# Seven products instead of eight for eleven hidden blocks of a state-space scan followed by a gated feed-forward layer

## The chip, the core and the metric

The kernel runs on one core of one Trainium2 chip. The core has TensorE (PE, matrix products into the accumulator memory PSUM), VectorE (DVE), ScalarE (ACT), GpSimd (POOL) and SyncE (SP, which issues DMA transfers here). Each engine works through its own queue in order, and the queues wait for one another through semaphores. Weight loads of TensorE have a row of their own in the profile (PEld). The metric is the device time of one execution in microseconds, as the median of several runs. All data is fp32.

## The reference: what is computed

First a chunked state-space scan (Mamba-2) over 4 batches, 8 heads, 768 positions, 32 channels a head and a state of 16. Its output, laid out as 3072 tokens of 256 numbers, goes through a feed-forward layer with a cosine gate:

```
M = (C_i . B_j) * exp(cum_i - cum_j), causal
y = M @ x + (C @ state) * exp(cum)          # per chunk, then the state is carried on
x = y as (3072, 256)
h = x @ w_in            # w_in  (256, 2048)
g = h * cos(h)
out = g @ w_out         # w_out (2048, 256)
```

## The kernel before

**Chunks and steps.** The sequence is cut into NC = 6 chunks of 128 positions (512 tokens over the four batches). The scan gives `yT[c]`, the transposed scan output of chunk c, as two halves u of 256 tokens each, with the 256 channels in two blocks k of 128. The feed-forward layer goes over each chunk in NF = 16 steps; step n = 16c + f. A step is one half u and one pair j of hidden blocks: 256 hidden numbers (two blocks e of 128) for 256 tokens (two blocks of 128). In the last chunk, steps 80 to 87 are the first half and 88 to 95 the second.

**What a step does.** `first(n)` (L650, products at L659) makes hp, the hidden block before the gate: four products of 256 columns into one PSUM bank, laid out as two blocks e by 256 tokens. It is eight block products of 128x128x128. `wind_k` (L664, ACT) rounds hp/2pi to whole turns k, `wind_w` (L669, DVE) takes the fraction w, `gate` (L679, ACT) turns w into the cosine, and `gated` (L683, DVE) multiplies it with hp into gT. Then `second(n - LAG)`, with LAG = 2, multiplies the gT of two steps ago with w_out.

**The second half in seven products.** From chunk 1 on, `second` is `seven` (L739). It forms the eight block products of a step out of seven (the scheme of Strassen and Winograd). For that it needs differences of the blocks of w_out, made once by POOL (`differ_w`, L695), and of the blocks of gT, made in every step by POOL (`differ`, L707: `gd`, three operations). The seven products are summed over the eight steps of a half in PSUM (`o[c, u]`). After the last of them ACT copies the accumulators out (`ps`, L776 and L777), four DVE adds (L784) put the output together, and SP writes it (L787). These adds wait in the list `unsummed` and are issued in a later step. The last step of all, 95, is done in plain products (`last_step`, L807), onto accumulators laid out for it.

**What sets the order.** The program is written with a manual schedule: each engine runs its instructions in the order in which the loop at L999 issues them. In a step of the last chunk that is: products of hp (PE), k (ACT), w (DVE), cosine (ACT), gT (DVE), differences of gT (POOL), then the adds of `unsummed` if they are due, then the seven products of step n - 2 (PE).

**PSUM.** It has eight banks: two for hp (tag "h"), two for accumulators (tag "o"), and two pairs (tag "scan") that serve the scan and are free once the scan of the last chunk is done. With two hp banks, gT of step n has to be made before hp of step n + 2 begins.

**SBUF used again.** `ms` are four buffers of 1024 numbers a partition. The scan uses the first two to its end, the other two only early on. The buffers with tag "words" held pieces of the weights while they were read in.

Of the kernel before, what the change touches and what calls it, by code (L numbers as in the profile page):

```python
# [8 lines left out]
FP32 = mybir.dt.float32  # L9
U32 = mybir.dt.uint32  # L10
I32 = mybir.dt.int32
AF = mybir.ActivationFunctionType
ALU = mybir.AluOpType
# [12 lines left out]
def kernel(  # L26
# [13 lines left out]
    V, ACT, G, PE = nc.vector, nc.scalar, nc.gpsimd, nc.tensor  # L40
# [3 lines left out]
    P = 128  # L44
    NC = S // P
    DM, DF = moe_w_in.shape
    KT = DM // P
    NF = DF // P
    TB = NB * P
# [3 lines left out]
    LAG = 2  # L53
# [15 lines left out]
    def bank(shape, name, tag):  # L69
        return psum.tile(shape, FP32, tag=tag, bufs=2, name=name)  # L70

    def pair(name):

        return psum.tile([P, 2, 4 * P], FP32, tag="scan", bufs=2, name=name)
# [570 lines left out]
    def turn_of(n):  # L645

        c, f = divmod(n, NF)
        return (f % 2, f // 2) if c == 0 else divmod(f, NJ)

    def first(n, between=None, tag="h"):  # L650
        c, f = divmod(n, NF)
        hp[n] = bank([P, TB], "hp", tag) if tag else pair("hp")[:, 0]

        u, j = turn_of(n)
        to_, y = hp[n].rearrange("p (e i) -> p e i", e=2), yT[c][:, u]
        for e in range(2):
            fs = slice((2 * j + e) * P, (2 * j + e + 1) * P)
            for k in range(KT):
                PE.matmul(to_[:, e], lhsT=w_in[:, k, fs], rhs=y[:, k],  # L659
                          start=(k == 0), stop=(k == KT - 1), skip_group_check=True)  # L660
            if between and e == 0:
                between()

    def wind_k(n):  # L664
        k = ffn.tile([P, TB], I32, tag="k", name="k")
        ACT.activation(k, hp[n], AF.Copy, bias=0.25, scale=INV_2PI)  # L666
        turns[n] = k

    def wind_w(n):  # L669
        k = turns[n]  # L670
        turns[n] = w = ffn.tile([P, TB], FP32, tag="w", name="w")
        V.scalar_tensor_tensor(out=w, in0=hp[n], scalar=INV_2PI, in1=k,  # L672
                               op0=ALU.mult, op1=ALU.subtract)

    def wind(n):
        wind_k(n)
        wind_w(n)

    def gate(n):  # L679
        cos = turns[n]  # L680
        ACT.activation(cos, cos, AF.Sin, bias=quarter, scale=TWO_PI)  # L681

    def gated(n):  # L683
        cos = turns.pop(n)
        gT[n] = ffn.tile([P, TB], FP32, tag="gT", bufs=LAG + 1, name="gT")
        V.tensor_tensor(out=gT[n], in0=hp.pop(n), in1=cos, op=ALU.mult)  # L686
        gT[n] = gT[n].rearrange("p (q m) -> p q m", q=4)
        if NF <= n < NC * NF - 1:
            differ(n)
# [5 lines left out]
    def differ_w(i, js):  # L695

        if i == len(wd):
            t = conv.tile([P, 2 * WC, 2], U32, tag="words", bufs=8, name="words")
            wd.append(t.rearrange("p a w -> p (a w)").bitcast(FP32)
                      .rearrange("p (j m) -> p j m", j=NJ))  # L700
        w11, w12, w21, w22 = (w4[:, js, e, h] for e in range(2) for h in range(2))
        a_ = (w12, w22, w22, w21)[i]
        b_ = (w11, w12, wd[0][:, js], wd[min(i, 2)][:, js])[i]
        op = ALU.add if i in (1, 2) else ALU.subtract
        G.tensor_tensor(out=wd[i][:, js], in0=a_, in1=b_, op=op)

    def differ(n):  # L707
# [5 lines left out]
        G.tensor_tensor(out=d[:, 2], in0=g[:, 0], in1=d[:, 0], op=ALU.subtract)  # L713
        G.tensor_tensor(out=d[:, 3], in0=g[:, 2], in1=d[:, 2], op=ALU.subtract)  # L714

    unit_rows = out.rearrange("(s q k i) m -> q k i s m", s=2, q=2, i=W)

    def second(n):
# [20 lines left out]
    def seven(n):  # L739

        c = n // NF
        u, j = turn_of(n)
        final = n >= NC * NF - NJ
        if j == 0:


            if final:
                lo, hi = (pair("o")[:, 0].rearrange("p (q m) -> p q m", m=P) for _ in range(2))
                mid = bank([P, 4, P], "o", "o")
                o[c, u] = (mid, lo, hi, {1: mid[:, 0], 6: mid[:, 1], 7: mid[:, 2], 5: mid[:, 3],  # L750
                                         2: lo[:, 0], 3: lo[:, 1], 4: hi[:, 0]})
            else:
                lo, hi = (bank([P, 4, P], "o", "o") for _ in range(2))
                o[c, u] = (lo, hi, {1: lo[:, 0], 6: lo[:, 1], 2: lo[:, 2], 7: hi[:, 0],
                                    5: hi[:, 1], 4: hi[:, 2], 3: hi[:, 3]})
        at = o[c, u][-1]
        g = gT.pop(n)
        if n == NC * NF - 1:
            last_step(g, *o[c, u][1:3])
            return  # L760
        d = gd.pop(n)
        w = {1: w4[:, j, 0, 0], 2: w4[:, j, 1, 0], 3: w4[:, j, 1, 1], 4: wd[3][:, j],
             5: wd[0][:, j], 6: wd[2][:, j], 7: wd[1][:, j]}
        a_ = {1: g[:, 0], 2: g[:, 2], 3: d[:, 3], 4: g[:, 3], 5: d[:, 0], 6: d[:, 2], 7: d[:, 1]}
        starts = (1, 2, 4) if final else (1, 7)
        for q in (1, 2, 6, 7, 5, 4, 3):
            PE.matmul(at[q], lhsT=a_[q], rhs=w[q], start=(j == 0 and q in starts),  # L767
                      stop=(j == NJ - 1), skip_group_check=True)
        if final and j == NJ - 2:
            shared(o[c, u][0])  # L770
        if j < NJ - 1:
            return

        sum_ = two.tile([P, 7, P], FP32, tag="sum", bufs=1, name="sum")
        ps = two.tile([P, 7, P], FP32, tag="ps", bufs=1, name="ps")
        ACT.copy(out=ps[:, 0:3], in_=o[c, u][0][:, 0:3])  # L776
        ACT.copy(out=ps[:, 3:7], in_=o[c, u][1])  # L777

        def rest():
            for dst, a_, b_ in ((sum_[:, 0:2], ps[:, 1:3], ps[:, 0:1]),  # L780
                                (sum_[:, 5:7], ps[:, 3:5], sum_[:, 0:1]),
                                (sum_[:, 3:5], ps[:, 5:3:-1], sum_[:, 5:6]),
                                (sum_[:, 2:3], ps[:, 6:7], sum_[:, 6:7])):
                V.tensor_tensor(out=dst, in0=a_, in1=b_.to_broadcast([P, dst.shape[1], P]),  # L784
                                op=ALU.add)
            for s in range(2):
                nc.sync.dma_start(out=unit_rows[s, 2 * c + u], in_=sum_[s * W:(s + 1) * W, 1:5].rearrange(  # L787
                                      "p (t h) m -> p t (h m)", t=2))

        unsummed.append(rest)  # L790

    unsummed = []
    shares_ = {}

    def shared(mid):
# [146 lines left out]

    AHEAD = 4

    def first_steps():

        grade("in", 1)
        for q in range(2):
            weights(1, q)
        states_of = []  # L950
        first(0, lambda: states_of.extend(finish0(1)))
        take_s1, add_s1 = states_of
        join("in", 1)
        rests = [grade("out", 0, later=True)]
        wind_k(0)
        take_s1()
        rests.pop()()
        wind_w(0)
        first(1)
        join("out", 0)  # L960
        wind_k(1)
        gate(0)
        wind_w(1)
        gate(1)
        gated(0)
        gated(1)
        first(2, tag=None)
        rests = [grade("in", 2, later=True)]
        wind_k(2)
        rests.pop()()  # L970
        clip_cut()
        wind_w(2)
        rests = [grade("out", 1, later=True)]
        join("in", 2)
        first(3, tag=None)
        gate(2)
        wind_k(3)
        rests.pop()()
        rests = [grade("in", 3, later=True)]
        gated(2)  # L980
        join("out", 1)
        second(0)
        wind_w(3)
        gate(3)
        rests.pop()()
        rests = [grade("out", 2, later=True)]
        join("in", 3)
        gated(3)
        second(1)
        clip_all()  # L990
        return add_s1, rests
# [7 lines left out]
    for n in range(AHEAD, NC * NF + LAG):  # L999
        c, f = divmod(n, NF)  # L1000
        if n < NC * NF:
# [10 lines left out]
                load_along(2, (2 * (n == NF), 2 * (n == NF) + 1))  # L1012
            for e, i in chunks_at(n, "along"):
                load_along(e + 1, (2 * i, 2 * i + 1))
            first(n)
            closing = f == NF - 1 and 1 <= c < NC - 1
            take_y = finish2(c + 1) if closing else None
            wind(n)
            if closing:
                take_y(0)  # L1020
            for e, s in chunks_at(n - 1, "turn"):
# [2 lines left out]
                turn_unit(k)  # L1024
            if n + 1 in piece:
                rests_of.append(grade(*piece[n + 1], later=True))
            gate(n)
            while len(rests_of) > (n == AHEAD):
                rest = rests_of.pop(0)
                if rest:  # L1030
# [14 lines left out]
            behind = [lambda k=k: weights(k, 1) for k in units_at(n - 1, 3)] + behind  # L1045
            if not joins and behind:
                behind.pop(0)()
            gated(n)
            if closing:
                take_y(1)  # L1050
            if n == NF + 7:
# [5 lines left out]
                exchange()  # L1057
            for do in behind:
                do()
            if f not in ((10, 11, 12) if c == 1 else (10, 11)):  # L1060
                for do in unsummed:
                    do()
                unsummed.clear()
# [2 lines left out]
                    weigh0(k)  # L1066
        for i, js in differ_at.get(n, ()):
            differ_w(i, js)
        if n == AHEAD + 1:
            second(AHEAD - LAG)  # L1070
        if n >= LAG and n != AHEAD:
# [53 lines left out]
```

## Time and profile before

| | |
|---|---|
| median of three runs | 368.21 us (367.43 to 368.46) |
| profiled execution, its own time | 367.37 us |
| its span, first to last instruction | 365.2 us |
| TensorE busy | 359.7 us (98%) |
| weight loads | 324.8 us (89%) |
| DVE busy | 249.6 us (68%) |
| POOL busy | 204.5 us (56%) |
| ACT busy | 177.8 us (49%) |
| granted TensorE clock, mean | 0.999 |
| hp of the last chunk's steps starts | at 305.36, then every 3.29 us |

In a line of the profile L659 is the line of the kernel, `hp<-yT,w_in` names the output and the inputs, x8 is a count. In groups, the busy time and the mean duration in nanoseconds follow, then the idle time of the engine just before and what ended it. In a timeline the first two numbers are start and duration in microseconds. Where a line of a timeline stands for several instructions, its duration is the sum or the union of theirs. Matmuls overlap one another, so the chain, which lays them end to end, gives the time that they take of TensorE.

### The profile page before, as it was taken

To read this page: it belongs to the slowest core of one execution; us is meant where nothing else is said; L and a number is where in the kernel's file an instruction comes from. 1 tells how busy PE (TensorE), PEld (TensorE's weight loads), DVE (VectorE), ACT (ScalarE), POOL (GpSimd) and SP (SyncE) were. 2 spreads that over 40 slices of the span, in tenths; PEclk is the share of its full clock that TensorE was granted. 3 is DMA by queue.
4 is the path that set the end of the run, shared out by engine and by line. 5 is a ranking of instruction groups with operands and counts; after the bars stand their busy time and mean duration, and the time that the engine had idled before them with its cause. 6 is when DMAs were issued, how large, how long until landed. Compare 5 with 4: busy or idle time off the path is not lost.

```text
span 365.2 us, 9749 instructions
## 1 busy us (share of the span) xinstructions
PE 359.7 (98%) x3902; PEld 324.8 (89%) x3902; DVE 249.6 (68%) x420; ACT 177.8 (49%) x324; POOL 204.5 (56%) x331
## 2 busy tenths in 40 slices
PE   8999999999999999999999999999999999999995
PEld 5788888888999999999989999989999999999995
DVE  7799998488868747967735977754876363644463
ACT  4588766454454355534345444335553534443442
POOL 6567666679766544447734456744355443554441
PEclk9999999999999999999999999999999999999999
DMA  8997865692664455316034210010000010010011
GB/s 146 294 334 154 203 139 72 105 129 64 133 98 65 92 106 72 69 39 121 9 56 62 47 50 22 2 44 5 22 11 0 2 31 2 2 29 3 0 29 31
DMA packets 97324, 26.39 MB, mean 72 GB/s; under 512 B 87328, under 2 KB 93184, under 8 KB 97280
## 3 DMA queue, kind: packets, MB, share of 16 engines
q1 hardware_dynamic: 96032, 25.38, 34.6%
q8 instruction: 31, 0.51, 0.6%
q10 hardware_dynamic: 1248, 0.39, 0.5%
q14 instruction: 13, 0.11, 0.1%
HBM read 22.36 MB, written 3.34 MB: 70 GB/s over the span
## 4 chain that ended last, share of the span: by engine, by line
PE 89%; DVE 4%; POOL 3%; ACT 2%; issue 2%; ACTq 0%; POOLq 0%; DVEq 0%
PE hp L659 42%; PE o L767 33%; PE o L729 5%; PE y L629 2%; PE g L603 1%; PE y L477 1%; DVE mag L261 1%; PE y L617 1%; DVE mag L263 1%; POOL gd L711 1%; PE g L456 1%; PE a_ps L364 1%; PE warm L84 1%; DVE w L672 1%; POOL gd L713 1%
## 5 line engine op out<-in xcount | busy, mean ns | idle before, releaser
L659 PE MATMUL hp<-yT,w_in 128*128 128x256 f32 x768 | 182.7, 381 | 0.3 <-DVE gT L686 0.3
L659 PEld LDWEIGHTS hp<-yT,w_in 128*128 128x128 f32 x768 | 139.5, 190 | 18.2 <-issue 1.0
L711 POOL TENSOR_TENSOR gd<-gT 128x256 f32<-128x256 f32 x79 | 59.8, 757 | 111.9 <-DVE gT L686 102.5
L672 DVE SCALAR_TENSOR_TENSOR w<-hp,k 128x512 f32<-128x512 f32 x96 | 66.1, 688 | 71.4 <-ACT k L666 71.3
L681 ACT ACTIVATE w<-w,quarter 128x512 f32<-128x512 f32 x96 | 69.4, 723 | 71.8 <-DVE w L672 71.5
L666 ACT ACTIVATE k<-hp 128x512 int32<-128x512 f32 x96 | 57.2, 596 | 94.3 <-PE hp L659 94.1
L686 DVE TENSOR_TENSOR gT<-hp,w 128x512 f32<-128x512 f32 x96 | 65.6, 683 | 35.1 <-ACT w L681 33.2
L767 PE MATMUL o<-words,gd 128*128 128x128 f32 x474 | 65.9, 275 | 0.1
L767 PEld LDWEIGHTS o<-words,gd 128*128 128x128 f32 x474 | 59.3, 192 | 0.3 <-POOL gd L713 0.3
L767 PEld LDWEIGHTS o<-w_out,gT 128*128 128x128 f32 x316 | 47.2, 191 | 4.1
L767 PE MATMUL o<-w_out,gT 128*128 128x128 f32 x316 | 48.4, 276 | 0.0
L714 POOL TENSOR_TENSOR gd<-gT,gd 128x128 f32<-128x128 f32 x79 | 44.0, 557 | 6.2
L713 POOL TENSOR_TENSOR gd<-gT,gd 128x128 f32<-128x128 f32 x79 | 38.1, 483 | 6.2
L767 PE MATMUL o<-words,gT 128*128 128x128 f32 x158 | 30.6, 275 | 0.0
L767 PE MATMUL o<-w_out,gd 128*128 128x128 f32 x158 | 30.6, 275 | 0.0
L729 PE MATMUL o<-w_out,gT 128*128 128x256 f32 x128 | 29.9, 379 | 0.0
L375 DVE TENSOR_TENSOR_SCAN lam<-arow,unit 128x512 f32<-128x512 f32 x20 | 28.0, 1400 | 0.0
L729 PEld LDWEIGHTS o<-w_out,gT 128*128 128x128 f32 x128 | 24.2, 190 | 3.3
L767 PEld LDWEIGHTS o<-words,gT 128*128 128x128 f32 x158 | 24.0, 192 | 0.0
L767 PEld LDWEIGHTS o<-w_out,gd 128*128 128x128 f32 x158 | 24.0, 192 | 0.0
L465 DVE TENSOR_TENSOR m<-g,lam 128x512 f32<-128x512 f32 x24 | 16.2, 681 | 0.7 <-PE g L456 0.5
L784 DVE TENSOR_TENSOR sum<-ps,sum 128x256 f32<-128x256 f32 (+1 forms) x27 | 15.1, 586 | 0.6
(109 smaller groups left out, 274.7 us busy)
## 6 DMA issues: line engine op xcount, KB each, us to landing
words<-in_moe_w_in_dram SPq DMA_DIRECT2D x8, 512.0 KB
words<-in_moe_w_out_dram SPq DMA_DIRECT2D x8, 512.0 KB
xr<-in_x_dram SPq DMA_DIRECT2D x24, 128.0 KB
arow<-a_cut SPq DMA_DIRECT2D x10, 256.0 KB
arow<-a_cut SPq DMA_DIRECT2D x10, 252.0 KB
out_dram<-sum SPq DMA_DIRECT2D x18, 128.0 KB
bc<-in_B_dram SPq DMA_DIRECT2D x24, 64.0 KB
blocks<-in_B_dram SPq DMA_DIRECT2D x16, 32.0 KB
```

The lines of the kernel that those rows point to most:

```text
L375: V.tensor_tensor_scan(out=lams[k][:, p, hs].rearrange(flat), data0=rows_.rearrange(flat), data1=unit0[:, hs].rearrange(flat), initial=0.0 ...
L465: V.tensor_tensor(out=m, in0=gs[k, q][:, :, 0:2 * P].rearrange("p k (s i) -> p k s i", s=2), in1=l, op=ALU.mult)
L659: PE.matmul(to_[:, e], lhsT=w_in[:, k, fs], rhs=y[:, k], start=(k == 0), stop=(k == KT - 1), skip_group_check=True)
L666: ACT.activation(k, hp[n], AF.Copy, bias=0.25, scale=INV_2PI)
L672: V.scalar_tensor_tensor(out=w, in0=hp[n], scalar=INV_2PI, in1=k, op0=ALU.mult, op1=ALU.subtract)
L681: ACT.activation(cos, cos, AF.Sin, bias=quarter, scale=TWO_PI)
L686: V.tensor_tensor(out=gT[n], in0=hp.pop(n), in1=cos, op=ALU.mult)
L711: G.tensor_tensor(out=d[:, 0:2], in0=g[:, 1:2].to_broadcast([P, 2, P]), in1=g[:, 3::-3], op=ALU.subtract)
L713: G.tensor_tensor(out=d[:, 2], in0=g[:, 0], in1=d[:, 0], op=ALU.subtract)
L714: G.tensor_tensor(out=d[:, 3], in0=g[:, 2], in1=d[:, 2], op=ALU.subtract)
L729: PE.matmul(o[c, u][:, t], lhsT=g[:, 2 * e + t], rhs=w_out[:, 2 * j + e], start=(j == e == t == 0), stop=(j == NJ - 1 and e == 1), skip_gr ...
L767: PE.matmul(at[q], lhsT=a_[q], rhs=w[q], start=(j == 0 and q in starts), stop=(j == NJ - 1), skip_group_check=True)
```

## The change

For eleven steps of the last chunk, n = 83 to 93 (`sevens`), hp is formed out of seven products of 128 columns (`first7`) instead of four of 256. The operands are blocks of w_in, differences of blocks of w_in (`wid`, made by POOL in sixteen operations during chunks 3 and 4), blocks of yT and differences of blocks of yT (`yd`, made by DVE after steps 79 and 80).

In such a step TensorE makes products 1 and 6, ACT copies product 1 out of the hp bank into `parts`, and TensorE goes on with 7, 5, 4 (into a bank beside) and 3, 2 (into the hp bank, 2 on top of 1). DVE then puts hp together in four adds, the last two of them writing into the hp bank. w of the step before stands in DVE's queue between the first of these adds and the other three; gT of the step before comes after them. So w, cosine and gT of such a step are issued one step later than before. hp gets a third bank: one of the pair tagged "scan", and from step 91 on one tagged "o".

The copies of the accumulators that are finished in a step of `sevens` go behind the copy of product 1 of the next step, through the list `finished`. The four adds over the accumulators of step 87 go to POOL, one in each of steps 90 to 93. Those of step 79 are issued in step 82, two before w and two after it. The seven products of the second half come in another order in these steps and in the last half, and the accumulators of the last half lie in other banks.

```diff
+    def differ_in(i, js):
...
+        g = [win4[:, k, js, e] for k in range(2) for e in range(2)]
+        a_ = (g[1], g[1], g[0], g[2])[i]
+        b_ = (g[3], g[0], wid[0][:, js], wid[min(i, 2)][:, js])[i]
+        G.tensor_tensor(out=wid[i][:, js], in0=a_, in1=b_, op=ALU.subtract)
+
+    def differ_y(c, i):
...
+            yd[c] = ms[2].rearrange("p (i u m) -> p i u m", i=4, u=2)
...
+        V.tensor_tensor(out=d[:, i], in0=a_, in1=b_,
+                        op=ALU.add if i in (1, 2) else ALU.subtract)
+
+    def first7(n, to_, at6, at):
...
+        w = {1: win4[:, 0, j, 0], 2: win4[:, 1, j, 0], 3: wid[3][:, j], 4: win4[:, 1, j, 1],
+             5: wid[0][:, j], 6: wid[2][:, j], 7: wid[1][:, j]}
...
+        dst = {6: at6, 1: to_[:, 0], 7: at[:, 0], 5: at[:, 1], 4: at[:, 2], 3: to_[:, 1],
+               2: to_[:, 0]}
...
+        for q in (1, 6):
+            product(q)
+        ACT.copy(out=parts[:, 0], in_=to_[:, 0])
+        while finished:
+            finished.pop()()
+        for q in (7, 5, 4, 3, 2):
+            product(q)
+        V.tensor_tensor(out=parts[:, 1], in0=at6, in1=parts[:, 0], **add)
+
+        def rest():
+            V.tensor_tensor(out=parts[:, 2:4], in0=at[:, 0:2],
+                            in1=parts[:, 1:2].to_broadcast([P, 2, P]), **add)
+            V.tensor_tensor(out=to_[:, 2:4], in0=at[:, 2:0:-1],
+                            in1=parts[:, 2:3].to_broadcast([P, 2, P]), **add)
+            V.tensor_tensor(out=to_[:, 1], in0=to_[:, 1], in1=parts[:, 3], **add)
...
-                lo, hi = (pair("o")[:, 0].rearrange("p (q m) -> p q m", m=P) for _ in range(2))
-                mid = bank([P, 4, P], "o", "o")
+                t = pair("o").rearrange("p b (q m) -> p b q m", m=P)
+                mid, hi = t[:, 0], t[:, 1]
+                lo = bank([P, 4, P], "o", "o")
...
-        for q in (1, 2, 6, 7, 5, 4, 3):
+        for q in ((1, 2, 4, 6, 7, 5, 3) if final else (1, 2, 7, 5, 6, 4, 3) if n in sevens else
+                  (1, 2, 6, 7, 5, 4, 3)):
...
+    sevens = range(NC * NF - 13, NC * NF - 2)
+    late, at_ = [], {}
+    quiet = (5, 6, 7, 8, 9, 13, 14, 15)
+
+    def first_of_seven(n):
+
+        i = n - sevens[0]
+        if i == -1:
+            at_["hp"] = pair("hp")[:, 0]
+            at_["m"] = pair("m").rearrange("p b (q m) -> p b q m", m=P)
+        if n == NC * NF - NJ + LAG + 1:
+            at_["hp"] = bank([P, TB], "hp", "o")
+        to_ = at_["hp"] if i % 3 == 2 else bank([P, TB], "hp", "h")
+        if n not in sevens:
+            first(n, to_=to_)
+            return
+        rest = first7(n, to_, at_["m"][:, 1, 0], at_["m"][:, 0])
+        if i:
+            wind_w(late[0])
+        rest()
...
+            if n not in sevens and n - 1 in sevens:
+                wind_w(n - 1)
+            if n - 1 in sevens:
+                gate(n - 1)
+            finish_late()
...
+            wind_k(n)
+            if n == sevens[0] - 1:
+                unsummed[0](range(0, 2))
+            if n not in sevens:
+                wind_w(n)
+            if n == sevens[0] - 1:
+                unsummed.pop()(range(2, 4))
...
+            for i in {sevens[0] - 4: (0, 2), sevens[0] - 3: (1, 3)}.get(n, ()):
+                differ_y(NC - 1, i)
+            if n in sevens and unsummed:
+                i = n - sevens[-1] + 3
+                unsummed[0](range(i, i + 1), G)
+                if i == 3:
+                    unsummed.pop()
...
+        if NC - 3 <= c < NC - 1 and f in quiet:
+            i, q = divmod((c - NC + 3) * len(quiet) + quiet.index(f), 4)
+            differ_in(i, slice(2 * q, 2 * q + 2))
```

More of the change, by code (lines that the diff above doesn't have):

```diff
@@ L648, in turn_of, with first @@
         return (f % 2, f // 2) if c == 0 else divmod(f, NJ)
-    def first(n, between=None, tag="h"):
+    def first(n, between=None, tag="h", to_=None):
         c, f = divmod(n, NF)
-        hp[n] = bank([P, TB], "hp", tag) if tag else pair("hp")[:, 0]
+        hp[n] = (to_ if to_ is not None else bank([P, TB], "hp", tag) if tag else
+                 pair("hp")[:, 0])
         u, j = turn_of(n)
@@ L714, in differ @@
         G.tensor_tensor(out=d[:, 3], in0=g[:, 2], in1=d[:, 2], op=ALU.subtract)
+    win4 = w_in.rearrange("p k (j e f) -> p k j e f", j=NJ, e=2)
+    wid, yd = [], {}
+    def differ_in(i, js):
+        if i == len(wid):
+            t = conv.tile([P, 2 * WC, 2], U32, tag="words", bufs=8, name="wid")
+            wid.append(t.rearrange("p a w -> p (a w)").bitcast(FP32)
+                       .rearrange("p (j f) -> p j f", j=NJ))
+        g = [win4[:, k, js, e] for k in range(2) for e in range(2)]
+        a_ = (g[1], g[1], g[0], g[2])[i]
+        b_ = (g[3], g[0], wid[0][:, js], wid[min(i, 2)][:, js])[i]
+        G.tensor_tensor(out=wid[i][:, js], in0=a_, in1=b_, op=ALU.subtract)
@@ new lines, in differ_y, with product @@
+    def differ_y(c, i):
+        if i == 0:
+            yd[c] = ms[2].rearrange("p (i u m) -> p i u m", i=4, u=2)
+        d = yd[c]
+        y11, y12, y21, y22 = (yT[c][:, :, k, h * P:(h + 1) * P] for k in range(2) for h in range(2))
+        a_ = (y12, y22, y22, y21)[i]
+        b_ = (y11, y12, d[:, 0], d[:, 2])[i]
+        V.tensor_tensor(out=d[:, i], in0=a_, in1=b_,
+                        op=ALU.add if i in (1, 2) else ALU.subtract)
+    def first7(n, to_, at6, at):
+        c, f = divmod(n, NF)
+        u, j = turn_of(n)
+        hp[n] = to_
+        to_ = to_.rearrange("p (q m) -> p q m", q=4)
+        w = {1: win4[:, 0, j, 0], 2: win4[:, 1, j, 0], 3: wid[3][:, j], 4: win4[:, 1, j, 1],
+             5: wid[0][:, j], 6: wid[2][:, j], 7: wid[1][:, j]}
+        d, y = yd[c][:, :, u], yT[c][:, u].rearrange("p k (h i) -> p k h i", h=2)
+        y_ = {1: y[:, 0, 0], 2: y[:, 1, 0], 3: y[:, 1, 1], 4: d[:, 3], 5: d[:, 0], 6: d[:, 2],
+              7: d[:, 1]}
+        dst = {6: at6, 1: to_[:, 0], 7: at[:, 0], 5: at[:, 1], 4: at[:, 2], 3: to_[:, 1],
+               2: to_[:, 0]}
+        def product(q):
+            PE.matmul(dst[q], lhsT=w[q], rhs=y_[q], start=(q in (6, 1, 7)), stop=True,
+                      skip_group_check=True)
+        parts = ms[3].rearrange("p (t q m) -> p t q m", t=2, q=4)[:, n % 2]
+        add = dict(op=ALU.add)
+        for q in (1, 6):
[12 more added lines that the diff above has]
+            V.tensor_tensor(out=to_[:, 1], in0=to_[:, 1], in1=parts[:, 3], **add)
+        return rest
@@ L775, in seven, with take, rest @@
         ps = two.tile([P, 7, P], FP32, tag="ps", bufs=1, name="ps")
[L776 to L786, printed above, removed]
+        lo, hi = o[c, u][0:2]
+        def take():
+            ACT.copy(out=ps[:, 0:3], in_=lo[:, 0:3])
+            ACT.copy(out=ps[:, 3:7], in_=hi)
+        if n in sevens:
+            finished.append(take)
+        else:
+            take()
+        def rest(of=range(4), eng=V):
+            for dst, a_, b_ in [((sum_[:, 0:2], ps[:, 1:3], ps[:, 0:1]),
+                                 (sum_[:, 5:7], ps[:, 3:5], sum_[:, 0:1]),
+                                 (sum_[:, 3:5], ps[:, 5:3:-1], sum_[:, 5:6]),
+                                 (sum_[:, 2:3], ps[:, 6:7], sum_[:, 6:7]))[i] for i in of]:
+                eng.tensor_tensor(out=dst, in0=a_, in1=b_.to_broadcast([P, dst.shape[1], P]),
+                                  op=ALU.add)
+            for s in range(2 if 3 in of else 0):
                 nc.sync.dma_start(out=unit_rows[s, 2 * c + u], in_=sum_[s * W:(s + 1) * W, 1:5].rearrange(
@@ L790, in seven @@
         unsummed.append(rest)
-    unsummed = []
+    unsummed, finished = [], []
     shares_ = {}
@@ L943, with finish_late @@
     AHEAD = 4
+    sevens = range(NC * NF - 13, NC * NF - 2)
[16 more added lines that the diff above has]
+        rest()
+    def finish_late():
+        while late:
+            n = late.pop()
+            gated(n)
     def first_steps():
@@ L1014 @@
                 load_along(e + 1, (2 * i, 2 * i + 1))
-            first(n)
+            if n + 1 in sevens or n in sevens or n - 1 in sevens:
+                first_of_seven(n)
+            else:
+                first(n)
+            if n not in sevens and n - 1 in sevens:
[3 more added lines that the diff above has]
+            finish_late()
             closing = f == NF - 1 and 1 <= c < NC - 1
             take_y = finish2(c + 1) if closing else None
-            wind(n)
+            wind_k(n)
[5 more added lines that the diff above has]
+                unsummed.pop()(range(2, 4))
             if closing:
@@ L1026 @@
                 rests_of.append(grade(*piece[n + 1], later=True))
-            gate(n)
+            if n not in sevens:
+                gate(n)
             while len(rests_of) > (n == AHEAD):
@@ L1047 @@
                 behind.pop(0)()
-            gated(n)
+            if n + 1 in sevens or n in sevens:
+                late.append(n)
+            else:
+                gated(n)
             if closing:
@@ L1059 @@
                 do()
-            if f not in ((10, 11, 12) if c == 1 else (10, 11)):
+            for i in {sevens[0] - 4: (0, 2), sevens[0] - 3: (1, 3)}.get(n, ()):
[5 more added lines that the diff above has]
+                    unsummed.pop()
+            if n not in sevens and f not in ((10, 11, 12) if c == 1 else (10, 11)):
                 for do in unsummed:
```

## The prediction

> **What bounds the kernel now.** I read the shares first, then the chain of waits, then one step of the timeline in the stretch that the change touches. TensorE is busy through nearly the whole span, and the stretch of the last chunk shows no gap at all. The columns of the second line are the stretch, its length, then the busy time of PE, weight loads, DVE, ACT and POOL, the granted clock and the DMA share:
>
> ```profile
> PE 359.7 (98%) x3902; PEld 324.8 (89%) x3902; DVE 249.6 (68%) x420; ACT 177.8 (49%) x324; POOL 204.5 (56%) x331
> ...
> 330.00:340.00 10.00, 10.00 (x69) 9.38 (x68) 4.15 (x6) 4.81 (x8) 5.04 (x10) 1.00 0.01 2
> ```
>
> The other engines are half idle there. The chain that ended last is pure TensorE (start, length, what):
>
> ```profile
> 318.52 1.73 PE hp L659 x8
> 320.25 1.56 PE o L767 x14
> 321.81 1.73 PE hp L659 x8
> ```
>
> A step of the last chunk lasts 3.29 us: 1.73 for hp (four fp32 products of 256 columns, which the profile shows as eight passes) and 1.56 for the seven products of the second half (14 passes of 128 columns). A pass costs 1.73/8 = 216 ns and 1.56/14 = 111 ns. So time is won only by taking passes away from TensorE, and kept only if what the change puts on ACT, DVE and POOL stays behind TensorE. The work of one step on those engines, from the timeline:
>
> ```profile
> 310.48 0.60 ACT L666 ACTIVATE k<-hp 128x512 int32<-128x512 f32 x1 [1.21 <-PE hp L659]
> ...
> 311.11 0.69 DVE L672 SCALAR_TENSOR_TENSOR w<-hp,k 128x512 f32<-128x512 f32 x1 [1.05 <-ACT k L666]
> ...
> 311.83 0.72 ACT L681 ACTIVATE w<-w,quarter 128x512 f32<-128x512 f32 x1 [0.76 <-DVE w L672]
> ...
> 312.66 0.69 DVE L686 TENSOR_TENSOR gT<-hp,w 128x512 f32<-128x512 f32 x1 [0.86 <-ACT w L681]
> ...
> 313.49 0.73 POOL L711 TENSOR_TENSOR gd<-gT 128x256 f32<-128x256 f32 x1 [1.50 <-DVE gT L686]
> ```
>
> From it: hp ends at 310.38, ACT starts 0.10 later; ACT and DVE follow each other within 0.04, POOL follows DVE within 0.14, and POOL needs 1.8 us for its three differences.
>
> **The gain.** In each of eleven steps (83 to 93) hp becomes seven products of 128 columns, 14 passes. The trace has that shape only in the second half; its row gives 14 x 111 = 1.56 us. Saved: 1.73 - 1.56 = 0.17 a step, 11 x 0.17 = 1.87 us.
>
> A rule speaks against counting on the arithmetic alone. The Trainium skill, "TensorE: Matmul & The Clock Gate", section LDWEIGHTS, prices a weight load by its columns, P/1.2, so 107 ns for 128, whatever streams behind it. Now eight loads hide behind passes of 216 ns; then 14 hide behind passes of 111, with 4 ns to spare. By the loads alone hp could take 14 x 107 = 1.50 us and save 2.6 us in all; by the row it takes 1.56. I take the row, since it carries loads and passes together. Seven products for eight (an eighth off the columns) thus give a tenth off the time.
>
> **The new work in a step.** ACT copies product 1 (128 columns out of PSUM). DVE adds 128 columns, 256, 256 and 128, and the last two write into PSUM. The near rows:
>
> ```profile
> L777 ACT COPY ps<-o 128x512 f32<-128x512 f32 x9 | 5.3, 588 | 0.0
> L776 ACT COPY ps<-o 128x384 f32<-128x384 f32 x9 | 4.1, 460 | 0.0
> L814 DVE TENSOR_TENSOR ob<-o,ps 128x256 f32<-128x256 f32 x2 | 0.8, 421 | 0.3 <-PE o L811 0.3
> L801 DVE TENSOR_TENSOR ps<-ps 128x256 f32<-128x256 f32 x1 | 0.4, 425 | 0.0
> L800 DVE TENSOR_TENSOR ps<-ps 128x128 f32<-128x128 f32 x1 | 0.3, 293 | 0.4 <-ACT ps L798 0.4
> ```
>
> The two copies differ by 128 ns per 128 columns, so one of 128 costs 0.20; the state copy of 128 columns with a scale (L489) took 0.40. I take 0.25. The adds cost 0.29, 0.42, 0.42, 0.29. Following one another on DVE, a dependent one starts 0.04 after the end of the one before it, an independent one 0.08 before (the four adds at 359.77, 360.10, 360.56, 360.77).
>
> DVE's queue in a step, as distances between starts: first sum 0.21, w of the step before 0.61, second sum 0.46, third 0.34, fourth 0.21, gT of the step before 0.61. Sum 2.44, against a step of 1.56 + 1.56 = 3.12. DVE doesn't become the bound, with 0.7 to spare.
>
> The loop that matters more runs through two engines: copy of product 1 (0.25 + 0.04), first sum 0.21, w 0.61, second 0.46, third 0.34, fourth with its end 0.33, the rounding k (0.60, the copy of the next step behind it on ACT starts 0.52 after k's start). Sum 2.76, under 3.12 by 0.36. With the copy at 0.40 it is 2.91.
>
> No row of this trace writes PSUM from DVE. The lower bound is nothing: the sums cost as into SBUF. For the upper, the Trainium skill, "Perfetto Trace Analysis", section Optimizing Scalar/DVE Operations, gives about 60 ns of access overhead for DVE on SBUF and 125 on PSUM, 65 ns more. The rows don't show that for reads: L814 reads PSUM and takes 421, L801 reads SBUF alone and takes 425. If all four sums paid it, the loop would be 3.02, still under 3.12; with the dear copy too it would be 3.17, 11 x 0.05 = 0.55 us late by the last step. I take nothing extra and keep 0.55 as the other end.
>
> **Where the new waits would bite.** Count from the first pass of hp. Product 1 is done at 0.22, the copy runs 0.32 to 0.57 (the k before it ends about 0.1), and products 3 and 2, which go into the copied bank, start at 1.12 and 1.34: half a microsecond of slack. Behind a late copy in ACT's queue stand the cosine of the step before and then k. Product 7 rewrites the bank that the second and third sums of the step before read; these end about 2.3, it starts at 3.12 + 0.45. gT of the step before is now made one step later, at 2.4 to 3.1; POOL then ends its differences by 5.0, that is 1.9 in the next step, where the second half starts at 1.56 but needs its last difference only as seventh product, at 2.9. A loop late by up to half a microsecond in all therefore costs TensorE nothing. The third hp bank is what lets gT come a step later.
>
> **Moved and added elsewhere.**
> - The copies of the finished accumulators (0.46 + 0.59) go behind the copy in step 90. They end about 1.6, where the cosine would begin anyway, since w ends about 1.5: nothing, and 0.1 if w is early.
> - The sums of the accumulators of step 87 go from DVE to POOL, one of four a step: 1.8 + 0.75 = 2.55 of 3.12. Their two output DMAs are issued by SP in step 94, about 353, ahead of the last ones at 361 as before.
> - The differences of y, four DVE adds at the ends of steps 79 and 80. DVE is idle from 305.63 to 307.82 and from 310.06 to 311.11. With both inputs in SBUF and POOL at work such an add took 0.41 and then 0.83 (L784 at 316.56 and 317.00), so two take 1.3 at most: hidden the first time, up to 0.2 over the second. What is late next is w, then the cosine, of step 81, whose gT has 1.9 us before its bank is wanted.
> - The sums of step 79 come ahead of w in step 82. Their second one ends about 314.5, k at 314.37: w and the cosine are 0.1 late, and the copy of step 83 stands behind that cosine and ends about 316.1. Product 3 wants it at 315.23 + 1.12 = 316.35. No stall; 0.3 if both lags add up.
> - The end. gT of step 95 ends at 359.41, 0.05 before the last products start at 359.46, so any lateness of ACT or DVE there would show. After step 93 the queue catches up: counted from step 94's hp, w and cosine of 93 end at 1.5, k of 94 starts at 1.8 when hp is done, gT of 94 ends about 4.7, and hp of 95 ends at 5.0. Nothing.
> - The new order of the products in the second half, and where its final accumulators lie, change no pass: nothing.
> - Sixteen differences of w_in on POOL in chunks 3 and 4, about 0.75 each. POOL is busy 5.0 of 10 us, and what it makes has 1.7 us in most steps. The tight place is steps 56 to 58 of chunk 3, where gd is ready 0.48 before its products start because DVE's scans hold POOL up. One such operation there makes the third product wait at worst 0.3. I take nothing.
>
> **Sum.** -1.87, with stalls between 0 and 1.1 (0.55 + 0.3 + 0.3) and 0 taken. The profiled execution had a span of 365.2 in 367.37 us; the span becomes 363.3. The median of the runs shown, 368.21, is 0.84 above that execution; taken from the median it is 366.3.
>
> **Rivals.**
> 1. The set-up or the switch costs most of the gain: POOL late at 56 to 58, the copy late at 83, the loop at 3.17. For it: a slack of 0.48 and one of 0.25. Against: every other one is over 1.5. With 1.1 us lost, 367.4, no change that can be told.
> 2. Slower: the sums collide with POOL. For it: the doubled L784 just named, and POOL differencing from 0.1 to 1.9 of each step, just where the first sums stand. Against: the new sums have one input in PSUM, and L465, of that kind, took 0.68 at 217.02 beside POOL at 217.25, no longer than alone. If all four grew by 0.41, 0.41, 0.25 and 0.25, DVE's queue would be 3.76 and set the step: 11 x (3.76 - 3.29) = 5.2 us more than before less 0.5 of slack, 372.9. It turns into a loss once DVE and ACT's loop is above 3.29 + 0.05.
> 3. The change doesn't do what it says: hp's 14 passes come to 1.73 because loads or waits between products show, 124 ns a pass. Against: L767 runs 14 with two releasers at 111. Then 368.2.
>
> **Numbers.** Forecast 0.79, rival 1 0.10, rival 2 0.07, rival 3 0.04. A measurement of this kernel tells 0.3%, 1.1 us, from no change. The forecast's own range is 365.8 to 366.9. Leaving out rivals 2 and 3, the range reaches to rival 1 and some of the run's own spread (1.0 us over three runs): 365.7 to 367.7. Faster 0.79, same 0.13 (rival 1 and three parts of rival 3), slower 0.08.
>
> **What would show it.** Right: the chain in the last chunk alternates 1.56 and 1.56 with no issue time; the new sums near 0.29 and 0.42; DVE about 2.8 busy of each 3.12 us; the first new copy (step 83) ending before product 3. Wrong: TensorE waiting for DVE or ACT between products 1 and 2, sums over 0.5 us, passes above 115 ns, or a gap of TensorE near 227 to 235 us.

## The result

The changed kernel took 367.15 us (366.41 to 368.35), the kernel before, beside it, 368.23 (367.24 to 369.01): a ratio of 0.9973, 95% interval 0.9963 to 0.9982. A second comparison, among the experiments below, gave 0.9995 (0.9982 to 1.0008), which alone can't be told from no change. The gain is less than forecast: 366.3 was predicted, 367.15 came, inside the range of 365.7 to 367.7.

The traces say where it went. Take the stretch from the first pass of hp in step 83 to the first pass of hp in step 94, the eleven steps that were changed. Before it lasted from 315.23 to 351.42, 36.19 us; eleven steps of 3.12 would be 34.3. It lasts 35.75 now, 315.22 to 350.97. Of 1.87 us of passes saved, 0.44 are left. The ends of the stretch in the two chains, before and now:

```profile
315.23 1.73 PE hp L659 x8
...
351.42 1.73 PE hp L659 x8
```

```profile
315.22 0.22 PE hp L759 x2
...
350.97 1.73 PE hp L660 x8
```

Ahead of the stretch nothing moved in these two executions, and from hp of step 94 to the end of the last addition it is 10.50 us in both. Behind the last addition the span runs on for 3.28 us before and 3.53 now, while the time that lies outside the span (the execution's own time less its span) falls from 2.17 to 1.74: 0.18 in favour of the change. 0.44 and 0.18 make up the difference between the two profiled executions, 367.37 and 366.74, to 0.01. The fall outside the span repeats: 1.74 to 1.84 in the 34 runs of the changed kernel, 2.09 to 2.76 in the 71 runs of before that are listed with the experiments. What makes it is not shown. Of the 1.08 us between the medians, 0.46 stay without a place in these traces.

The totals of the changed kernel's page; TensorE's busy time falls by 0.8, DVE's rises by 12 and POOL's by 14:

```profile
PE 358.9 (98%) x3968; PEld 325.7 (89%) x3968; DVE 261.7 (72%) x464; ACT 179.4 (49%) x335; POOL 218.6 (60%) x351
```

The chain of the changed kernel through steps 84 to 86 (start, length, what). hp is now in three pieces: product 1, then 6, 7, 5, 4 (tile m), then 3 and 2:

```profile
318.44 0.22 PE hp L759 x2
318.66 0.89 PE m L759 x8
319.56 0.45 PE hp L759 x4
320.00 1.56 PE o L835 x14
321.57 0.22 PE hp L759 x2
321.79 0.89 PE m L759 x8
322.68 0.71 PE hp L759 x4
323.39 1.56 PE o L835 x14
324.95 0.22 PE hp L759 x2
325.18 0.89 PE m L759 x8
326.07 0.45 PE hp L759 x4
```

In step 84 hp takes 0.22 + 0.89 + 0.45 = 1.56, as forecast. In step 85 the last piece takes 0.71. It does so in every second step: the excess over 0.45 is 0.10, 0.26, 0.23, 0.23, 0.20 and 0.19 in steps 83, 85, 87, 89, 91 and 93, together 1.21. Four of the second halves, in steps 90 to 93, take 1.59 or 1.60 instead of 1.56, 0.14 more. 34.38 (eleven steps of 3.125) + 1.21 + 0.14 = 35.73: the whole stretch, to 0.02.

The timelines of DVE, ACT and the weight loads around step 85, which starts at 321.57:

```profile
319.66 0.29 DVE L771 TENSOR_TENSOR m<-m 128x128 f32<-128x128 f32 x1 [1.01 <-PE m L759]
319.87 0.68 DVE L673 SCALAR_TENSOR_TENSOR w<-hp,k 128x512 f32<-128x512 f32 x1
320.47 0.41 DVE L774 TENSOR_TENSOR m<-m 128x256 f32<-128x256 f32 x1
320.99 0.43 DVE L776 TENSOR_TENSOR hp<-m 128x256 f32<-128x256 f32 x1
321.46 0.30 DVE L778 TENSOR_TENSOR hp<-hp,m 128x128 f32<-128x128 f32 x1
321.66 0.68 DVE L687 TENSOR_TENSOR gT<-hp,w 128x512 f32<-128x512 f32 x1
```

```profile
321.87 0.60 ACT L667 ACTIVATE k<-hp 128x512 int32<-128x512 f32 x1 [0.50 <-PE hp L759]
322.36 0.26 ACT L766 COPY m<-hp 128x128 f32<-128x128 f32 x1
```

```profile
322.68 0.30 PEld L759 LDWEIGHTS hp<-yT,wid 128*128 128x128 f32 x2 [0.18 <-ACT m L766]
```

The first sum of step 84 needs products 1 and 6, which are done 0.45 after the step's start at 318.44. It starts at 1.22, after DVE sat idle for 1.01 until TensorE was done with tile m: product 4 ended at 319.56. w, which needs nothing of this, stands behind it. So k starts at 321.87, 3.43 after its step began and not 2.56, to which the prediction's distances add up. The copy of step 85 behind it on ACT ends at 322.62, 1.05 into the step. Product 3's weight load is due at 0.84 (in step 84, which has no wait, it starts at 319.28; the load shows 0.11 ahead of its pass, and the pass 0.17 ahead of where the chain lays it). It starts at 322.68, 1.11 into the step and 0.27 late, and products 3 and 2 with it. The late step is longer by the wait, so the next copy comes earlier in its own step and nothing waits there: hence every second step.

### The profile page after: what moved, and what is told of

Its sections match the earlier page's. It is cut to its first block, busy times and chain, and to the rows that moved or that the text cites. A ratio compares the mean times of both kernels' runs of the same rounds, so it can differ in the third digit from the quotient of the medians.

```text
span 365.0 us, 9976 instructions
## 1 busy us (share of the span) xinstructions
PE 358.9 (98%) x3968; PEld 325.7 (89%) x3968; DVE 261.7 (72%) x464; ACT 179.4 (49%) x335; POOL 218.6 (60%) x351
## 4 chain that ended last, share of the span: by engine, by line
PE 87%; DVE 4%; POOL 3%; ACT 2%; issue 2%; DMA 1%; SPq 0%; ACTq 0%; POOLq 0%; DVEq 0%
PE hp L660 37%; PE o L835 33%; PE o L795 5%; PE m L759 3%; PE hp L759 2%; PE y L629 2%; PE g L603 1%; DMA bc<-in_B_dram 1%; DVE mag L261 1%; PE y L477 1%; PE y L617 1%; DVE mag L263 1%; POOL gd L714 1%; POOL gd L712 1%; PE g L456 1%
## 5 line engine op out<-in xcount | busy, mean ns | idle before, releaser
L660 PE MATMUL hp<-yT,w_in 128*128 128x256 f32 x680 | 161.9, 382 | 0.4 <-DVE gT L687 0.4
L660 PEld LDWEIGHTS hp<-yT,w_in 128*128 128x128 f32 x680 | 123.8, 190 | 16.4 <-issue 1.0
L714 POOL TENSOR_TENSOR gd<-gT,gd 128x128 f32<-128x128 f32 x79 | 40.6, 514 | 6.2
L715 POOL TENSOR_TENSOR gd<-gT,gd 128x128 f32<-128x128 f32 x79 | 40.3, 511 | 6.2
L271 POOL TENSOR_TENSOR w_out<-mag,last 128x512 uint32<-128x512 uint32 x8 | 10.2, 1271 | 9.1 <-DVE mag L263 9.1
```

The lines of the kernel that those rows point to most:

```text
L660: PE.matmul(to_[:, e], lhsT=w_in[:, k, fs], rhs=y[:, k], start=(k == 0), stop=(k == KT - 1), skip_group_check=True)
```

## The experiments

The theory from that reading, A: the loop through copy, sums, k and copy is too long, because the first sum waits for the last product into its tile and holds up w and the other sums. Rivals: the pattern is an accident of one execution (B); the gain was eaten by the set-up or the switch (C); DVE is full (D); the first sum waits for something else (E); the passes themselves are dearer (F). All stretches below are from hp of step 83 to hp of step 94, read from the chain.

**The same kernel again** (after_again).

> The changed kernel once more. Theory A: products 3 and 2 of hp wait in every second step for the copy of product 1, which stands behind k on ACT; k is late because the first sum waits until the last product into the bank beside is done, 0.65 later than reckoned, and w and the other sums stand behind it. Then the stretch from hp of step 83 to hp of step 94 lasts 35.7 to 35.8 us again, with waits of about 0.2 us in every second step, and the ratio is near 0.997. Theory B (the waits are an accident of one execution): another pattern of waits, a stretch of 34.3 to 35.2.

Measured: 317.67 to 353.41, 35.74, waits in the same steps and of the same sizes to 0.03. B is out. The ratio, 0.9995 (0.9982 to 1.0008), was not the 0.997 expected. In this execution step 83 began 2.45 us later than in the other one, with the same program ahead of it. What lies ahead of the stretch moves from one execution to the next by more than the change is worth: it began between 314.99 and 318.10 in the ten traces of before, after and the experiments. In the latest of them (the kernel eight, below) the chain between 36 and 54 us goes over loads and stores: 6.12 us of the load of w_out, 3.62 of storing a, 2.09 of loading it again. So the stretch is the sharper measure here. This movement is the likely reason why the two comparisons stand apart; one trace of each can't show it.

**w ahead of the first sum** (w_first). The first sum moves from before w to behind it on DVE; one line:

```diff
-        V.tensor_tensor(out=parts[:, 1], in0=at6, in1=parts[:, 0], **add)

         def rest():
+            V.tensor_tensor(out=parts[:, 1], in0=at6, in1=parts[:, 0], **add)
             V.tensor_tensor(out=parts[:, 2:4], in0=at[:, 0:2],
```

> On DVE w of the step before goes ahead of the first sum; nothing else is changed. Theory A: the sums then end 0.4 to 0.5 us earlier in the step, k starts near 2.95 instead of 3.41 after the start of the step, the next copy ends near 0.65, before product 3 wants it; no waits, a stretch of 34.3 to 34.5 us (eleven steps of 3.12) and a ratio near 0.993 to 0.995. Theory C (the gain was eaten outside this loop, by the set-up or the switch): the stretch stays at 35.7, ratio 0.997. Theory D (DVE itself is full): no change either, with DVE busy without pauses.

Measured: 315.42 to 349.90, 34.48, ratio 0.9948 (0.9934 to 0.9962); 365.85 us where the changed kernel took 367.46 on the same chip. DVE's and ACT's timelines in step 86, which starts at 324.89:

```profile
325.33 0.69 DVE L673 SCALAR_TENSOR_TENSOR w<-hp,k 128x512 f32<-128x512 f32 x1
326.11 0.29 DVE L773 TENSOR_TENSOR m<-m 128x128 f32<-128x128 f32 x1
326.44 0.42 DVE L774 TENSOR_TENSOR m<-m 128x256 f32<-128x256 f32 x1
326.97 0.43 DVE L776 TENSOR_TENSOR hp<-m 128x256 f32<-128x256 f32 x1
327.44 0.30 DVE L778 TENSOR_TENSOR hp<-hp,m 128x128 f32<-128x128 f32 x1
```

```profile
327.83 0.60 ACT L667 ACTIVATE k<-hp 128x512 int32<-128x512 f32 x1 [1.05 <-PE o L835]
328.33 0.27 ACT L766 COPY m<-hp 128x128 f32<-128x128 f32 x1
```

w fills the time in which DVE had stood still, the first sum still starts at 1.22, and k at 2.94 instead of 3.43. The copy ends 0.58 into the next step. Only the wait of step 83 is left (0.54 for 0.45). C and D are out as what ate the gain of the stretch: the same work on DVE, in another order, gives back 1.27 us of it.

**The copy ahead of k** (copy_before_k). On ACT, k of a step moves behind the copy of the next:

```diff
         ACT.copy(out=parts[:, 0], in_=to_[:, 0])
+        while unwound:
+            wind_k(unwound.pop())
...
-            wind_k(n)
+            if n in sevens:
+                unwound.append(n)
+            else:
+                wind_k(n)
```

After step 93, k is issued just ahead of its w.

> The order on ACT is turned round: the copy of product 1 goes ahead of k of the step before; DVE's order stays. Theory A: the copy ends about 0.6 after the start of each step, k of the step before at 1.15, still ahead of its w at 1.43; no waits of products 3, a stretch of 34.3 to 34.5, ratio 0.993 to 0.995. Theories C and D: 35.7 and 0.997.

Measured: 314.99 to 350.40, 35.41, ratio 0.9965 (0.9952 to 0.9977): less than expected. Its chain in steps 87 and 88:

```profile
327.71 0.22 PE hp L759 x2
327.93 0.89 PE m L759 x8
328.83 0.45 PE hp L759 x4
329.27 1.70 PE o L837 x14
330.97 0.22 PE hp L759 x2
331.19 0.89 PE m L759 x8
332.08 0.45 PE hp L759 x4
332.53 1.56 PE o L837 x14
```

The waits of product 3 are gone from step 84 on, as A says, but seven second halves now take 1.69 to 1.71, 0.95 more in all. They wait for POOL. gT of step 85 starts only at 327.80, as step 87 begins, and POOL's third difference ends at 330.43; the last product of step 87's second half, which works on step 85, needs it:

```profile
327.80 0.68 DVE L687 TENSOR_TENSOR gT<-hp,w 128x512 f32<-128x512 f32 x1
...
329.97 0.46 POOL L715 TENSOR_TENSOR gd<-gT,gd 128x128 f32<-128x128 f32 x1
...
330.49 0.48 PE L837 MATMUL o<-w_out,gd 128*128 128x128 f32 x2
```

So the late first sum has a second cost behind the first one: it also makes gT late, and taking away the wait for the copy lays that bare. Moving w ahead cures both: in w_first gT starts 2.75 into the step (327.64) instead of 3.22.

**A longer copy** (extra_copy). ACT makes a copy that nothing uses, ahead of the one that counts:

```diff
+        ACT.copy(out=parts[:, 3], in_=ident)
         ACT.copy(out=parts[:, 0], in_=to_[:, 0])
```

> ACT copies 128 columns from SBUF (0.30, which nothing uses) ahead of the copy of product 1 in each of the eleven steps. Theory A: k starts 3.41 after its step, the copy follows, so two steps together last 6.43 plus the added 0.22: a step of 3.33 instead of 3.25 on average, the stretch 36.6 to 37.0, the time 0.9 to 1.3 us over the changed kernel's (ratio to before about 1.000). Theories C and D: ACT is half idle, so nothing, 0.997.

Measured: 315.57 to 352.43, 36.86, ratio 1.0009 (1.0001 to 1.0017), 0.8 us over the changed kernel on the same chip, a little under the 0.9 expected. ACT was busy about half the time, and 0.3 us more of it in a step still lengthen the stretch by 1.1. The chain of this kernel runs through k and the copies in steps 85, 87, 89, 91 and 92 (here in step 85; L766 is the extra copy, L767 the one that counts):

```profile
322.40 0.07 ACT k L667
322.47 0.43 issue
322.90 0.29 ACT m L766
323.19 0.18 ACT m L767
323.36 0.04 issue
323.41 0.71 PE hp L759 x4
```

**Product 6 in a tile of its own** (six_apart). For steps 83 to 89:

```diff
-            at_["hp"] = pair("hp")[:, 0]
-            at_["m"] = pair("m").rearrange("p b (q m) -> p b q m", m=P)
+            at_["six"] = pair("six")[:, 0, 0:P]
+            m = pair("m")
+            at_["hp"] = m[:, 1]
+            at_["m"] = m.rearrange("p b (q m) -> p b q m", m=P)
...
-        rest = first7(n, to_, at_["m"][:, 1, 0], at_["m"][:, 0])
+        rest = first7(n, to_, at_["six"] if i < 7 else at_["m"][:, 1, 0], at_["m"][:, 0])
```

> Product 6 goes into a tile of its own in steps 83 to 89 (its bank is taken from the pair that held the third hp bank, which moves beside products 7, 5, 4); DVE's and ACT's orders are the changed kernel's. Theory A, first sum held by the last of products 7, 5, 4 because they share a tile with product 6: the first sum then starts near 0.6 after the start of the step instead of 1.22, and w, the sums and k come about 0.5 earlier; no waits of products 3 in steps 84 to 89 (in 90 to 93 they stay, 0.2 every second step); the stretch from hp of step 83 to hp of step 94 34.7 to 35.1 instead of 35.7; ratio 0.995 to 0.997. Theory E, the first sum waits for something else (PSUM write to read takes that long): it starts at 1.2 as before, 35.7.

Measured: 315.28 to 352.72, 37.44, ratio 1.0023 (1.0009 to 1.0037). The part that tells A from E came as A says; the stretch did not. In step 84, which starts at 318.49, DVE's timeline has:

```profile
319.05 0.29 DVE L771 TENSOR_TENSOR m<-six,m 128x128 f32<-128x128 f32 x1 [0.57 <-ACT m L766]
319.26 0.68 DVE L673 SCALAR_TENSOR_TENSOR w<-hp,k 128x512 f32<-128x512 f32 x1
```

The first sum starts at 0.56 and waits for the copy, no longer for TensorE. So it had been the shared tile: the program's waits treat the two banks of a pair as one thing. But the third hp bank now shares a tile with products 7, 5 and 4, and there the program's waits hit in the same way. In this kernel's chain, step 86:

```profile
325.42 0.22 PE six L759 x2
325.65 0.95 PE m L759 x6
...
328.42 0.69 DVE gT L687
329.11 0.04 issue
329.15 0.94 PE m L759 x6
```

Product 7 of step 87 waits for gT of step 85, which reads hp in the bank beside it; in steps 85 and 88, whose own hp lies in that bank, it waits for the copy of product 1. I had not counted that when I wrote 34.7 to 35.1. A division of the eight banks that keeps both apart, product 6 and the third hp bank, was not tried.

**The passes alone** (seven_alone). The seven products go straight into the hp bank; the copy of product 1 and the four sums are left out, so hp is not the true hidden block.

```diff
+        dst = {1: to_[:, 0], 2: to_[:, 0], 3: to_[:, 1], 4: to_[:, 2], 5: to_[:, 3], 6: to_[:, 3],
+               7: to_[:, 3]}
...
         def rest():
+            pass
```

> The seven products go straight into the hp bank and are not put together: the copy of product 1 and the four sums are left out, so hp is not the right hidden block; all else stays. It measures the fourteen passes alone. Theory A: 11 steps of 3.12 to 3.13, a stretch of 34.3 to 34.4, ratio 0.9945 to 0.9955, the same as with w first. Theory F (the passes of hp are slower than those of the second half, or the set-up costs): a stretch above 34.8.

Measured: 316.05 to 350.44, 34.39, ratio 0.9952 (0.9936 to 0.9969). F is out; the chain:

```profile
319.17 1.56 PE hp L767 x14
320.74 1.56 PE o L831 x14
```

**Eight products again** (eight), with everything else of the change kept:

```diff
+        def all_(e):
+            for k in range(KT):
...
+                PE.matmul(hp[n].rearrange("p (e i) -> p e i", e=2)[:, e], lhsT=w_in[:, k, fs],
+                          rhs=yT[c][:, u, k], start=(k == 0), stop=(k == KT - 1),
```

> Undoes the seven products alone: the eleven steps take eight again, without copy and sums; the differences of w_in and y, the third hp bank, w and gT one step later, and the sums on POOL all stay. Theory A: these cost and bring nothing, the stretch is 36.2 and the ratio 0.999 to 1.001. Theory C (set-up or switch eat the gain): over 1.002.

Measured: 318.10 to 354.29, 36.19, the length before to the hundredth; ratio 0.9997 (0.9981 to 1.0013). C is out for the time as a whole, to within that interval. The differences of w_in and y, the third bank, the shifted w and gT and the sums on POOL cost nothing and bring nothing.

**w ahead of the first sum, beside seven_alone** (w_first_again).

> The kernel with w ahead of the first sum, beside seven_alone on the same chip. Theory A: a stretch of 34.4 to 34.5 again and a ratio of 0.994 to 0.9955, within 0.001 of seven_alone: nothing of the new work shows on TensorE any more. Otherwise the gap between the two is what copy and sums still cost.

Measured: 315.70 to 350.19, 34.49, ratio 0.9933 (0.9919 to 0.9946), below the expected ratio, and 0.0019 from seven_alone's instead of within 0.001; the two intervals overlap. In the stretch, copy and sums cost 0.10 us over the bare passes, the wait of step 83. This version beats the kernel before in both comparisons, and the changed kernel in the one in which both ran (365.85 and 367.46 us).

## Why the prediction was right, and where it was off

That the time came into the range is in part luck. The stretch, which is all that the forecast counted on, gave 0.44 of 1.87 us; taken from the median before, that is 367.8, just outside the range. The rest of the 1.08 came from outside the stretch, 0.18 of it from behind the last addition, and no step of the prediction names it.

- **The gain on TensorE** (1.87, from 14 passes of 111 ns): right. The bare passes measure 36.19 - 34.39 = 1.80. The row of the second half was the right one to take, against the price of the loads alone (2.6).
- **The set-up and the switch at nothing**: right. Kernel eight shows 36.19, and POOL's sixteen differences held up no product in chunks 3 and 4. The copy of step 83 was forecast to end about 316.1 and ended at 316.11; the wait of 0.10 came because product 3's weight load is due 0.28 ahead of its pass's place in the chain, at 316.06, which I had left out.
- **The durations of the new work**: right. Copy 0.26 (0.25 taken), sums 0.29, 0.42, 0.43 and 0.30. Writing into PSUM cost DVE about 10 ns (means of 433 and 300 ns, where the prediction's rows into SBUF have 425 and 293). The 65 ns of the Trainium skill's "Perfetto Trace Analysis", section Optimizing Scalar/DVE Operations, kept as the dear end, did not show on a write any more than on a read. Nor did POOL double the sums (rival 2).
- **The loop through copy, sums and k, under 3.12 by 0.36**: this step failed. k starts 3.43 after its step, not 2.56. Of the 0.87, 0.61 are the first sum (1.22 instead of 0.61), 0.06 lie between the second and the third, 0.13 between the third and the fourth, which follow one another like dependent ones, though the fourth does not use the third's result, and 0.07 are the handing over to ACT. I had the bounds of the durations from both sides and none for the wait: I took the first sum to wait for the product that it reads, where the program makes it wait for all products into the tile. So the mechanism of rival 1, "the loop", decided, at a place and for a reason that rival 1 didn't name.
- **"Half a microsecond of slack"**: off as well. It was 1.12 - 0.57; the weight load of product 3 is due at 0.84, and the copy of step 85 ended at 1.05.
- **gT at 2.4 to 3.1**: it came at 3.22 to 3.90 (the line of 321.66, counted from step 84's start at 318.44). POOL's slack of 1.0 was gone with it: 0.03 to 0.04 were lost in each of four steps here, and 0.14 in seven once the first wait was out of the way. The prediction looked only at POOL's last difference. In steps 90 to 93 product 6, which wants the second one, stands fourth in the second half (in step 90 that difference ended at 339.89 and the product's weight load started at 339.94), so the new order was not free there.
- **The end** and the forecast signs: DVE was busy 7.98 us of the ten from 320 to 330 and had not become the bound; TensorE waited for ACT, which I had named as what would show the forecast wrong. Of 1.87 forecast, 0.44 stayed in the stretch.

## What to carry to other kernels

When a step is shortened on the engine that bounds, price the loop that comes back to it through the other engines by what each instruction waits for in the program, not by what it reads: two banks in one tile were one thing here, and it held the first sum back by 0.66 us in each step (1.22 against 0.56). In a queue that runs in order, put the instruction that is ready (w) ahead of the one that waits (the first sum); here one line was worth 1.27 us of the stretch, nearly three times what the change had brought there. And when waits come in every second step, look for a loop a little longer than the step: the late step pays for two.

## What the runs showed of the hardware

In ten of the eleven steps k started 0.09 to 0.12 after the end of the fourth sum, which DVE writes into PSUM (321.76 and 321.87 in step 84; the same in w_first). The cosine started 0.03 or 0.04 after the end of w, which DVE writes into SBUF, but for one step of each kernel (0.10 and 0.19). That the memory makes the difference was not tested by itself. The part ahead of the stretch, with the same program, took up to 3.1 us more in one execution than in another, 318.10 against 314.99.
